# Folding w_phi into key weights by tiles of 64 rows and 64 columns, in a two-layer Hedgehog and Mish kernel

## Chip, cores and metric

The kernel runs on 1 core of one Trainium2 chip, in float32. The metric is the device time of one execution in microseconds. A matmul whose operands have the type fp32r stands in the trace as one record; one with plain float32 operands stands as two.

## The reference

Two layers, each an attention block and a dense block, on x of 2048 rows and 640 columns. Attention has 32 heads of 20.

```python
q, k, v = layernorm(x) @ wqkv                      # 32 heads of 20 each
pq = einsum("bhsd,hdf->bhsf", q, w_phi);  pk = the same of k
phi_q = concat(softmax(pq), softmax(-pq));  phi_k = the same of pk
kv = phi_k^T v;  z = sum of phi_k
x = x + (phi_q kv / (phi_q z + 1e-6)) @ wo
x = x + mish(layernorm(x) @ w1 + b1) @ w2
```

## The kernel before

Rows are worked in 8 blocks of 256 (two tiles of 128). To keep precision with fp32r matmuls, weights and activations are split into a high part (ScalarE copies to fp32r) and a low part (another engine subtracts), and each product is three matmuls: high by high, high by low, low by high (`project_half`, L418).

At the start of layer one w_phi is folded into the query and key weights once, so that no block has to multiply by it: the transposed weight rows are the stationary operand and w_phi, laid out as blocks on a diagonal, is the moving one. Of each head's 20 columns the last is subtracted from the other 19 first (`shift_phi`, on POOL), which a softmax does not see. The result lies in PSUM; `fold_high` copies it to the high weights on ACT, `fold_low` subtracts on DVE for the low weights. Query weights are folded first; the key weights (`fold_phi`) in two portions, ahead of the second values and ahead of the first keys of block 0, whose order is q0, v0, v1, k0, q1, k1.

`features` makes the features of a tile of queries or keys: copy from PSUM (ACT, L436 or L439), maximum and minimum (DVE, L443), the difference to the maximum (L444, on POOL for queries and on DVE for keys), the difference to the minimum (DVE, L446), exp (ACT, L449), the sums and reciprocals (DVE, L454, L455), and the scaling (POOL, L457). A query tile is then turned on DVE (L525) and stored to HBM in four pieces of e_d (SP, L528). Query tiles lie in two buffers by turns, so query i + 2 may be written only when the stores of query i have landed; the first to write is the MEMSET of L434 on POOL.

All DMAs are issued by SP, in its order. Each engine's order comes from a scheduler, held in part by `tc.issue_after`. In block 0 of layer one, waiting generators are moved on by `advance`; `last_fold` holds the last subtraction of the fold.

Of the kernel before, what the change touches and what calls it, by code (L numbers as in the profile page):

```python
# [16 lines left out]
P = 128  # L17
# [27 lines left out]
def kernel(  # L45
# [22 lines left out]
    def mm_tile():  # L68
        return psum.tile([P, 2, 512], F32, tag="mm", name="mm", bufs=2)
# [179 lines left out]
    def load_raw(which, ts=range(6)):  # L249

        raw = []
        for t in ts:
            rows = 120 if t < 4 else 80
            if t < 5:
                r = wts.tile([P, D], F32, tag=f"r2{'hl'[which]}{5 + t}", name=f"raw{which}{t}")
            else:
                r = r2_wide(10 + which, F32)[:, 0]

            n = P if t < 5 else rows
            c0 = which * D + (t * 120 if t < 5 else D - rows)  # L260
            nc.sync.dma_start(r[:n], wqk_t[c0:c0 + n, :])
            raw.append((r, rows))
        return raw
# [26 lines left out]
        last_fold[0] = nc.vector.tensor_tensor(ws[k][1][:, cs], ps[:, :cs.stop - cs.start],  # L290
                                               ws[k][0][:, cs].bitcast(F32), op=ALU.subtract).ins

    def fold_phi(ws, bd, raw, parts):

        for n in range(0, len(parts), 2):
            mm = mm_tile() if n < 4 else None
            pair = list(zip(parts[n:n + 2], [one_tile(), one_tile()] if mm is None else [mm[:, 0], mm[:, 1]]))
            with tc.issue_after(last_product[0]):
                for (k, c), ps in pair:
                    for t in range(3 * c, 3 * c + 3):  # L300
                        fold_part(ps, k, t, bd, raw)
            for end in (fold_high, fold_low):
                for (k, c), ps in pair:
                    end(ws, ps, k, c)


    def norm_stats(t, xt):

# [158 lines left out]
    def attend_first(layer, x_src, first):  # L467
# [46 lines left out]

        def queries(xts, i, ps=None):
            e = query_tile(i)
            yield from features(project(xts, i % BT, q_ws, 0, w=QC) if ps is None else ps, e, True)

            b, t = divmod(i, BT)
            if i == NT - BT - 1:  # L520
                yield
                with tc.issue_after(last_recip[0]):
                    nc.vector.transpose(e, e)
            else:
                nc.vector.transpose(e, e)  # L525
            dst = e_d[b].rearrange("(j f) (t q s) -> t q f j s", f=32, t=BT, s=32)
            for q in range(4):
                ins = nc.sync.dma_start(dst[t, q], e[32 * q:32 * q + 32].rearrange("f (j s) -> f j s", s=32))  # L528
                last_store[0] = ins.ins
                if b == NB - 1:  # L530
                    yield
# [15 lines left out]
        if first is None:  # L547
            with written():
                xt = fetch(x_src, 0)
                bd = big_tile()[:120, :720].rearrange("p (t c) -> p t c", t=6)  # L550
                nc.sync.dma_start(bd[:, :3], phi_bd[:, :3])
                raw_q = load_raw(0, range(3))

                nc.vector.memset(bd[:80, 5, :80], 0.0)
                nc.sync.dma_start(bd[:40, 5, :40], phi_bd[80:120, 4, 80:120])
                nc.sync.dma_start(bd[40:80, 5, 40:80], phi_bd[:40, 5, :40])
                nc.sync.dma_start(bd[:, 3:5], phi_bd[:, 3:5])
                shift_phi(bd, slice(0, 3))
                raw_q += load_raw(0, range(3, 6))
                kv_ws = [r1_pair(k) for k in range(KD)]  # L560
                raw_v = [fetch_v(k) for k in range(KD)]
                raw = load_raw(1)
                early = fetch(x_src, 1)
                mvs = [norm_stats(t, xt) for t in range(BT)]
                norm_scale(0, mvs)
                shift_phi(bd, slice(3, 5))
                shift_phi(bd, 5)

                q_ws = [r2_pair(k) for k in range(KD)]
                mm = [mm_tile(), mm_tile()]  # L570
                pcs = [one_tile(), mm[0][:, 0], mm[0][:, 1], mm[1][:, 0], mm[1][:, 1]]
                for t in range(3):
                    for k in range(KD):
                        fold_part(pcs[k], k, t, bd, raw_q)
                xn = [row_tile() for _ in range(BT)]
                act(xn[0], xt[:, 0, :], AF.Identity, bias=stats[:, 0, 1, 0:1], scale=stats[:, 0, 0, 0:1])
                nc.vector.tensor_scalar(xn[1], xt[:, 1, :], stats[:, 0, 0, 1:2], stats[:, 0, 1, 1:2],
                                        op0=ALU.mult, op1=ALU.add)

                def highs(c, ks):  # L580
                    for k in ks:
                        fold_high(q_ws, pcs[k], k, c)

                def lows(c, ks):
                    for k in ks:
                        fold_low(q_ws, pcs[k], k, c)

                def make_v(k, low):
                    split(kv_ws[k][0][:, D:2 * D], kv_ws[k][1][:, D:2 * D], raw_v[k], low)

                def half(c, ks):
                    project_half(q0[c], nxt, 0, q_ws, 0, c, ks, w=QC)

                highs(0, (0, 1, 2))
                lows(0, (0,))
                nxt = Transposed(xn)
                nxt.turn(one_tile())
                nxt.high()
                lows(0, (1, 2))
                nxt.lower()  # L600
                highs(0, (3, 4))
                pcs[0], pcs[1] = one_tile(), one_tile()
                for k in (0, 1):
                    fold_part(pcs[k], k, 3, bd, raw_q)
                nxt.turn(one_tile())
                for t in (4, 5):
                    for k in (0, 1):
                        fold_part(pcs[k], k, t, bd, raw_q)
                last = mm_tile()
                nxt.turn(last[:, 0])  # L610
                nxt.high()
                nxt.high()
                lows(0, (3, 4))
                nxt.lower()
                nxt.lower()
                highs(1, (0, 1))
                q0 = [one_tile()]
                half(0, (0, 1))
                mm = mm_tile()
                pcs[2], pcs[3] = mm[:, 0], mm[:, 1]  # L620
                for k in (2, 3):
                    for t in range(3, 6):
                        fold_part(pcs[k], k, t, bd, raw_q)
                lows(1, (0, 1))
                half(0, (2, 3))
                make_v(0, nc.gpsimd)
                highs(1, (2, 3))
                lows(1, (2, 3))
                pcs[4] = last[:, 1]
                for t in range(3, 6):  # L630
                    fold_part(pcs[4], 4, t, bd, raw_q)
                half(0, (4,))
                make_v(1, nc.gpsimd)
                highs(1, (4,))
                lows(1, (4,))
                q0.append(one_tile())
                half(1, range(KD))
                for k in (2, 3, 4):
                    make_v(k, nc.vector)
            nc.sync.dma_start(mask, bass.AP(tensor=head_mask.tensor, offset=head_mask.offset,  # L640
                                            ap=[[1, 120], [120 * (DH + 1), 3]]))
        else:
            nxt, kv_ws, turn = first
            with tc.issue_after(last_load[0]):
                load_k_weights(kv_ws)
            q_ws = load_q_weights()
        for b in range(NB):
# [15 lines left out]
            for n, (kind, t) in enumerate(order):  # L663
                t = int(t)
                i = b * BT + t
                if b == 0 and layer == 0 and n in (2, 3):
                    if n == 2:
                        advance()
                    fold_phi(kv_ws, bd, raw, ((0, 0), (1, 0), (2, 0), (3, 0)) if n == 2 else
                             ((4, 0), (0, 1), (1, 1), (2, 1), (3, 1), (4, 1)))  # L670
                if b == 0 and n == (1 if layer else 3):
                    kva = one_tile()
                    nc.vector.memset(kva[:, :360], 0.0)
# [13 lines left out]
                if b == 0 and not layer:  # L687
                    with tc.issue_after(last_product[0]):
                        next(g)
                    with (tc.issue_after(last_fold[0]) if n > 3 else nullcontext()):  # L690
                        advance()
                    if n == 1:
                        xt = fetch_normed(1)
                elif b == NB - 1 and n == 3:
                    advance()
                    next(g)
                else:
                    next(g)
                    if layer and b == 0 and n == 0:
                        turn()  # L700
                    advance()
# [449 lines left out]
```

## Time and profile before

| | us |
|---|---|
| median of 3 runs | 1353.56 (1352.92 to 1353.92) |
| the profiled execution | 1354.08 |
| its span, first to last instruction | 1352.1 |
| PE busy | 1346.0 |
| DVE busy | 1040.4 |
| ACT busy | 576.6 |
| POOL busy | 480.6 |

The granted TensorE clock was 1.000 of full speed. In a timeline row the columns are: start and busy time in us, engine, line, operation, what it writes and reads, shape, count, and in brackets the idle time of the engine before it and what ended it. A row of the table by windows gives the stretch, its length, the busy time of each engine with its count of instructions (PE, PEld, DVE, ACT, POOL), the granted clock, the DMA engines' mean busy share and GB/s. A row of waits gives the engine, its tile and line, what it waited for, the sum in us, the number and the longest.

### The profile page before, as it was taken

How to read it: one execution, taken by the hardware profiler on the slowest of the kernel's cores; microseconds unless marked ns; L12 is line 12 of the kernel's file. 1: busy time of each engine (PE TensorE's matmuls, PEld its weight loads, DVE VectorE, ACT ScalarE, POOL GpSimd, SP SyncE). 2: the span in 40 equal slices, each digit the busy share in tenths (PEclk: the TensorE clock that was granted, in tenths of full speed). 3: DMA queues.
4: the chain of work that ended last, by engine and by line, in shares of the span. 5: the costliest groups of instructions: out<-in, count | busy, mean ns of one | idle time of the engine just before them, and what ended most of it. 6: DMA issues, size and time to landing. Idle time of an engine off the chain costs nothing. (4 is left out here: it accounts for less than half of the span.)

```text
span 1352.1 us, 31029 instructions
## 1 busy us (share of the span) xinstructions
PE 1346.0 (100%) x12896; PEld 1337.5 (99%) x12896; DVE 1040.4 (77%) x1737; ACT 576.6 (43%) x974; POOL 480.6 (36%) x479
## 2 busy tenths in 40 slices
PE   9999999999999999999999999999999999999999
PEld 9999999999999999999999999999999999999998
DVE  6888888876787877778768788789768776676775
ACT  5444444222454554445443334332236444444443
POOL 3365554434322222222226655634351211111112
PEclk9999999999999999999999999999999999999999
DMA  9554444698713443234474444548974221233200
GB/s 334 165 119 103 99 99 102 170 287 284 214 25 87 117 118 78 61 98 113 144 221 108 113 97 90 95 95 270 278 253 121 79 73 38 87 98 98 65 35 21
DMA packets 352694, 174.12 MB, mean 129 GB/s; under 512 B 287513, under 2 KB 324105, under 8 KB 352553
## 3 DMA queue, kind: packets, MB, share of 16 engines
q1 hardware_dynamic: 352553, 172.14, 46.6%
q8 instruction: 101, 1.65, 0.5%
q14 instruction: 40, 0.33, 0.1%
HBM read 106.23 MB, written 65.86 MB: 127 GB/s over the span
## 5 line engine op out<-in xcount | busy, mean ns | idle before, releaser
L952 POOL TENSOR_TENSOR ol<-big,ol 128x512 fp32r<-128x512 f32 (+1 forms) x98 | 131.9, 1346 | 471.8 <-ACT ol L951 406.1
L977 PE MATMUL mm<-r2h,ol 128*128 128x320 f32 x1240 | 296.1, 309 | 0.0
L926 PE MATMUL one<-xtl,r1h 128*128 128x256 f32 x960 | 268.2, 279 | 0.0
L926 PE MATMUL one<-xth,r1l 128*128 128x256 f32 x960 | 268.0, 279 | 0.0
L926 PE MATMUL one<-xth,r1h 128*128 128x256 f32 x960 | 265.8, 279 | 0.0
L977 PEld LDWEIGHTS mm<-r2h,ol 128*128 128x128 f32 x1240 | 212.4, 188 | 0.0
L977 PE MATMUL mm<-r2l,ol 128*128 128x320 f32 x620 | 191.2, 309 | 0.0
L418 PE MATMUL mm<-r1h,xth 128*128 128x304 f32 (+1 forms) x600 | 184.9, 308 | 1.1 <-ACT r L135 1.1
L418 PE MATMUL mm<-r1h,xtl 128*128 128x304 f32 (+1 forms) x600 | 183.8, 306 | 0.2 <-POOL xtl L355 0.2
L418 PE MATMUL mm<-r1l,xth 128*128 128x304 f32 (+1 forms) x600 | 184.0, 307 | 0.0
L926 PEld LDWEIGHTS one<-xtl,r1h 128*128 128x128 f32 x960 | 180.4, 188 | 0.0
L926 PEld LDWEIGHTS one<-xth,r1l 128*128 128x128 f32 x960 | 180.4, 188 | 0.0
L926 PEld LDWEIGHTS one<-xth,r1h 128*128 128x128 f32 x960 | 179.6, 188 | 0.0
L941 DVE TENSOR_SCALAR big<-big 128x512 f32<-128x512 f32 (+1 forms) x98 | 55.4, 565 | 121.2 <-ACT big L939 116.8
L939 ACT ACTIVATE big<-one,b1s 128x256 f32<-128x256 f32 x192 | 80.9, 468 | 101.4 <-PE one L926 101.2
L951 ACT ACTIVATE ol<-big 128x512 fp32r<-128x512 f32 (+1 forms) x98 | 60.9, 622 | 136.5 <-DVE big L950 136.4
L457 POOL TENSOR_TENSOR r<-r,r 128x1280 f32<-128x1280 f32 x32 | 77.4, 2420 | 112.3 <-DVE r L455 88.9
L977 PEld LDWEIGHTS mm<-r2l,ol 128*128 128x128 f32 x620 | 116.4, 188 | 0.0
L943 ACT ACTIVATE big<-big,two 128x512 f32<-128x512 f32 (+1 forms) x98 | 70.1, 715 | 105.5 <-DVE big L942 105.4
L418 PEld LDWEIGHTS mm<-r1h,xth 128*128 128x128 f32 x600 | 112.8, 188 | 2.0 <-ACT r L135 1.4
L418 PEld LDWEIGHTS mm<-r1h,xtl 128*128 128x128 f32 x600 | 112.8, 188 | 0.3 <-POOL xtl L355 0.3
L418 PEld LDWEIGHTS mm<-r1l,xth 128*128 128x128 f32 x600 | 112.8, 188 | 0.1
(167 smaller groups left out, 3138.5 us busy)
## 6 DMA issues: line engine op xcount, KB each, us to landing
e_d<-r SPq DMA_DIRECT2D x128, 160.0 KB, 4.0
big<-e_d SPq DMA_DIRECT2D x30, 640.0 KB, 7.5
x_d<-xt SPq DMA_DIRECT2D x23, 640.0 KB, 5.0
xt<-x_d SPq DMA_DIRECT2D x22, 640.0 KB, 4.7
n_d<-xn SPq DMA_DIRECT2D x168, 80.0 KB, 2.2
xt<-in_x SPq DMA_DIRECT2D x16, 640.0 KB, 4.9
xn<-x_d SPq DMA_DIRECT2D x28, 320.0 KB, 4.5
v<-n_d SPq DMA_DIRECT2D x30, 256.0 KB, 3.0
```

The lines of the kernel that those rows point to most:

```text
L418: last_product[0] = nc.tensor.matmul(ps[:, :w], a[:, sl], r, start=(k == 0 and n == 0), stop=(k == KD - 1 and n == 2)).ins
L457: ins = scale.tensor_tensor(eg, eg, r.unsqueeze(2).to_broadcast([P, 2 * H, DH]), op=ALU.mult).ins
L926: nc.tensor.matmul(ph[:, j, :], l, r, start=(n == 0), stop=(n == 3 * KD - 1))
L939: exps[0] = nc.scalar.activation(part(ta, 0)[:, j - js.start], ph[:, j, :], AF.Exp, bias=b1s[:, 2 * pr + j:2 * pr + j + 1]).ins
L941: nc.vector.tensor_scalar_min(e, e, E_CAP)
L943: nc.scalar.activation(r, n, AF.Ln, bias=two)
L951: nc.scalar.activation(ah[:, js], n, AF.Copy)
L952: nc.gpsimd.tensor_tensor(al[:, js], n, ah[:, js].bitcast(F32), op=ALU.subtract)
L977: ins = nc.tensor.matmul(pys[t][c][:, :HC], (ah, ah, al)[n][:, j, t * P:(t + 1) * P], w, start=(f == 0 and n == 0), stop=(f == KF - 1 and ...
```

## The change

Four edits. First, the key rows are loaded shifted by 4 rows, so that three heads lie in partitions 4 to 63 and three in 64 to 123, and w_phi is loaded a second time in that layout (`load_phi_halves`), with zeros in rows 0 to 3, and subtracted by `shift_phi`. Second, `fold_keys` takes the place of `fold_phi`: 22 products for each of five k, each of at most 64 rows by 64 columns, the two row halves into different PSUM banks, the column halves into different partitions; a k is evacuated with one instruction over both banks and one for the last two heads (three for k = 4). Third, in block 0 the `advance` at n = 3, which turns query 0, is placed behind the last subtraction of the fold. Fourth, in layer two L444 of query tile 2 (the first of block 1) is done by DVE.

```diff
-            n = P if t < 5 else rows
-            c0 = which * D + (t * 120 if t < 5 else D - rows)
+            if which:
+                n = P if t < 5 else 64
+                c0 = D + (120 * t - 4 if t < 5 else D - n)
...
+    def load_phi_halves():
+
+        ph = pair_tile(F32).rearrange("p a s -> p (a s)")[:, :360].rearrange("p (t c) -> p t c", t=6)
+        nc.vector.memset(ph, 0.0)
+        for s in range(2):
+            nc.sync.dma_start(ph[4 + 60 * s:64 + 60 * s, :5], phi_bd[60 * s:60 * s + 60, :5, 60 * s:60 * s + 60])
+        nc.sync.dma_start(ph[24:64, 5, :40], phi_bd[:40, 5, :40])
+        return ph
+
+    def fold_keys(ws, ph, raw, ks):
+
+        w = 3 * DL
+        for k in ks:
+            mm = mm_tile() if k < KD - 1 else None
+            ps = [one_tile(), one_tile()] if mm is None else [mm[:, 0], mm[:, 1]]
             with tc.issue_after(last_product[0]):
+                for t in range(6):
+                    heads = 3 if t < 5 else 2
+                    for s in range(2 if t < 5 else 1):
+                        rows = slice(64 * s, 64 + 60 * s)
+                        for c in range(2):
+                            last_product[0] = nc.tensor.matmul(
+                                ps[s][64 * c:64 * c + 64, t * w:t * w + heads * DL].rearrange("p (j d) -> p j d", d=DL),
+                                raw[t][0][rows, k * P + 64 * c:k * P + 64 * c + 64],
+                                ph[rows, t, :heads * DH].rearrange("p (j d) -> p j d", d=DH)[:, :, :DL],
+                                start=True, stop=True).ins
...
+            outs.append((ps[0][:, 5 * w:5 * w + 2 * DL], *ends))
+            for src, hi, lo in outs:
+                nc.scalar.activation(hi, src, AF.Copy)
+            for src, hi, lo in outs:
+                last_fold[0] = nc.vector.tensor_tensor(lo, src, hi.bitcast(F32), op=ALU.subtract).ins
...
-            yield from features(project(xts, i % BT, q_ws, 0, w=QC) if ps is None else ps, e, True)
+            yield from features(project(xts, i % BT, q_ws, 0, w=QC) if ps is None else ps, e, not layer or i != BT)
...
                 raw = load_raw(1)
+                ph = load_phi_halves()
                 early = fetch(x_src, 1)
...
                     make_v(k, nc.vector)
+                shift_phi(ph, slice(0, 6))
...
-                    fold_phi(kv_ws, bd, raw, ((0, 0), (1, 0), (2, 0), (3, 0)) if n == 2 else
-                             ((4, 0), (0, 1), (1, 1), (2, 1), (3, 1), (4, 1)))
+                    fold_keys(kv_ws, ph, raw, (0, 1) if n == 2 else (2, 3, 4))
...
-                    with (tc.issue_after(last_fold[0]) if n > 3 else nullcontext()):
+                    with (tc.issue_after(last_fold[0]) if n > 2 else nullcontext()):
                         advance()
```

The diff moves line numbers by 29 or 30 from `features` on: L444 becomes L473, L446 L475, L457 L486, L525 L554, L528 L557.

On DVE, behind the statistics of block 1 (r1l are the low key weights, r_361 and r_367 query 0), before:

```order
L454 TENSOR_REDUCE r<-r_361 128x64
L290 TENSOR_TENSOR r1l_167<-mm,r1h_166 128x342
L290 TENSOR_TENSOR r1l_169<-mm,r1h_168 128x342
L455 RECIPROCAL r<-r 128x64
L290 TENSOR_TENSOR r1l_171<-mm,r1h_170 128x342
L290 TENSOR_TENSOR r1l_173<-mm,r1h_172 128x342
L525 STREAM_TRANSPOSE r_361<-r_361 128x1280
L673 MEMSET one 128x360
L290 TENSOR_TENSOR r1l_175<-mm,r1h_174 128x342
```

and after, from the subtractions of k = 2 on:

```order
L334 TENSOR_TENSOR r1l_171<-mm,r1h_170 128x2x5x57
L334 TENSOR_TENSOR r1l_171<-mm,r1h_170 128x38
L703 MEMSET one 128x360
L334 TENSOR_TENSOR r1l_173<-mm,r1h_172 128x2x5x57
L334 TENSOR_TENSOR r1l_173<-mm,r1h_172 128x38
L334 TENSOR_TENSOR r1l_175<-one,r1h_174 128x5x57 x2
L334 TENSOR_TENSOR r1l_175<-one,r1h_174 128x38
L554 STREAM_TRANSPOSE r_367<-r_367 128x1280
```

The turn of query 0 has moved behind all subtractions of the fold.

On SP, where the folded weights are stored (wp_d) and wo is loaded, before:

```order
L164 DMA raw_1069<-in_wo 128x640
L464 DMA xt<-in_x 128x1280
L528 DMA e_d_116<-r_361 32x40x32 x4
L230 DMA wp_d<-r1h_166 128x608
L230 DMA wp_d<-r1l_167 128x608
```

and after, from the last key weights that are stored before the queries:

```order
L164 DMA raw_1159<-in_wo 128x640
L164 DMA raw_1155<-in_wo 128x640
L230 DMA wp_d<-r1h_174 128x608
L230 DMA wp_d<-r1l_175 128x608
L557 DMA e_d_116<-r_367 32x40x32 x4
L493 DMA xt<-in_x 128x1280
```

The four stores of query 0 stand behind all ten stores of key weights and the two further loads of wo.

On POOL, after (r_670 is query 1, r_820 query 2, ol the halves of w_phi):

```order
L463 MEMSET r_367 128x32
L463 MEMSET big 128x32 x2
L282 TENSOR_TENSOR ol<-ol 128x18x19
L473 TENSOR_TENSOR r_367<-r_367,m 128x32x20
L349 TENSOR_SCALAR ve<-mv 128x1 x2
L350 TENSOR_TENSOR stats<-ve,neg_half 128x2
L352 TENSOR_SCALAR stats<-mv,stats 128x1 x2
L486 TENSOR_TENSOR r_367<-r_367,r 128x1280
L463 MEMSET r_670 128x32
L463 MEMSET r_820 128x32
L473 TENSOR_TENSOR r_670<-r_670,m 128x32x20
```

The subtraction on the halves is new, ahead of the first query's difference; the MEMSETs of queries 1 and 2 stood ahead of query 1's difference before too.

More of the change, by code (lines that the diff above doesn't have):

```diff
@@ L257, in load_raw @@
                 r = r2_wide(10 + which, F32)[:, 0]
-            n = P if t < 5 else rows
-            c0 = which * D + (t * 120 if t < 5 else D - rows)
+            if which:
+                n = P if t < 5 else 64
+                c0 = D + (120 * t - 4 if t < 5 else D - n)
+            else:
+                n = P if t < 5 else rows
+                c0 = t * 120 if t < 5 else D - rows
             nc.sync.dma_start(r[:n], wqk_t[c0:c0 + n, :])
@@ L291, in fold_low @@
                                                ws[k][0][:, cs].bitcast(F32), op=ALU.subtract).ins
[L293 to L297, printed above, removed]
-            with tc.issue_after(last_product[0]):
[L299 to L304, printed above, removed]
+    def load_phi_halves():
[5 more added lines that the diff above has]
+        return ph
@@ new lines, in fold_keys @@
+    def fold_keys(ws, ph, raw, ks):
[3 more added lines that the diff above has]
+            ps = [one_tile(), one_tile()] if mm is None else [mm[:, 0], mm[:, 1]]
+            with tc.issue_after(last_product[0]):
+                for t in range(6):
[8 more added lines that the diff above has]
+                                start=True, stop=True).ins
+            pairs = [x[:, :10 * w].rearrange("p (t s d) -> p s t d", s=2, d=w) for x in ws[k]]
+            ends = [x[:, 10 * w:QK] for x in ws[k]]
+            if mm is None:
+                outs = [(ps[s][:, :5 * w].rearrange("p (t d) -> p t d", d=w), *(x[:, s] for x in pairs))
+                        for s in range(2)]
+            else:
+                outs = [(mm[:, :, :5 * w].rearrange("p s (t d) -> p s t d", d=w), *pairs)]
+            outs.append((ps[0][:, 5 * w:5 * w + 2 * DL], *ends))
[3 more added lines that the diff above has]
+                last_fold[0] = nc.vector.tensor_tensor(lo, src, hi.bitcast(F32), op=ALU.subtract).ins
```

## The prediction

> **What bounds the kernel now.** I read the head of the page first, then the table of what TensorE waited for, then the timelines of all engines around the two stretches that the diff touches.
>
> ```profile
> span 1352.1 us, 31029 instructions
> PE 1346.0 (100%) x12896; PEld 1337.5 (99%) x12896; DVE 1040.4 (77%) x1737; ACT 576.6 (43%) x974; POOL 480.6 (36%) x479
> ...
> PE mm L418 <- ACT r L135: 1.1, 1, 1.1
> PE mm L418 <- POOL xtl L355: 0.2, 1, 0.2
> ```
>
> TensorE is the bound: it is busy for 1346.0 of 1352.1 us, and inside the program it waits for other engines in only two places worth a word, 1.1 and 0.2 us, both in layer two. So there are three ways to move the time: fewer microseconds of matmuls, the end of those waits, or a new wait. The rest of the kernel matters only by its slack.
>
> **The fold on TensorE.** Before, the 30 products of the key fold stand as 60 records in two stretches.
>
> ```profile
> 24.23 2.83 PE L270 MATMUL mm<-big,raw 120*128 120x114 f32 x24
> 26.83 0.39 PE L418 MATMUL one<-r1h,xth 128*128 128x320 f32 x1
> ...
> 31.31 1.24 PE L270 MATMUL mm<-big,raw 120*128 120x114 f32 x10
> ...
> 35.28 0.60 PE L338 MATMUL one<-ident,xn 128*128 128x128 f32 x4
> 35.64 0.38 PE L418 MATMUL mm<-r1h,xth 128*128 128x304 f32 x1
> ```
>
> They take 26.83 - 24.23 = 2.60 and 35.28 - 31.31 = 3.97 us, 6.57 together. After, there are 110 products of 64 rows by 64 columns with 57 moving columns (38 in the last), 220 records. The nearest rows are the products that already use tiles of columns.
>
> ```profile
> 71.95 1.48 PE L511 MATMUL one<-big,ol 128*21 128x40 f32 x128
> 73.36 0.42 PE L418 MATMUL mm<-r1l,xth 128*128 128x320 f32 x1
> ...
> 246.72 1.39 PE L802 MATMUL mm<-kvb,big 120*64 120x63 f32 x40
> 247.93 0.27 PE L802 MATMUL mm<-kvb,ol 80*64 80x42 f32 x4
> ```
>
> L802, two tiles of 64 columns with 63 moving columns, starts 40 records in 1.21 us: 60 ns for a pair. L511, four tiles, starts 128 records in 1.41 us: 11 ns for one. So tiles side by side overlap; tiles one below the other occur in no row. If they overlap too, each k costs ten groups of four and two pairs, 12 x 60 ns = 0.72 us, and five cost 3.6 us. About 0.2 us for each of the two changes of tile shape (an estimate) leaves a saving of 2.6 us. If they don't, 110 pairs at 60 ns are 6.6 us and nothing is saved. I take the first, since L511 shows that four can be in flight.
>
> The Trainium skill, "TensorE: Matmul & The Clock Gate", section "Wait — 56ns, not 53.3ns?", says that starts of small matmuls never come closer than about 25 ns. By that rule 220 records would take 5.5 us and the saving would be 1.1 us; the 11 ns of L511 disagree, and the measurement decides.
>
> **What the first key projection then waits for.** The saving counts only if L418 at 35.64 can start earlier. New on its path are three loads of w_phi in halves, the subtraction on them (`shift_phi`, POOL), and their place: on POOL the subtraction stands ahead of the first query's L444, and the loads stand between the key rows and the x tile of block 1.
>
> ```profile
> 44.00:48.00 4.00, 4.00 (x32) 4.00 (x31) 3.03 (x6) 0.95 (x2) 1.28 (x1) 1.00 1.02 376
> ...
> 5.45 0.76 POOL L278 TENSOR_TENSOR big<-big 120x342 f32<-120x342 f32 x1 [4.16 <-DMA big<-in_phi_bd]
> ...
> 21.86 1.28 POOL L444 TENSOR_TENSOR r<-r,m 128x640 f32<-128x640 f32 x1 [0.59 <-DVE m L443]
> ...
> 24.59 1.67 DVE L311 BATCH_NORM_STATS2 bn<-xt 128x6 f32<-128x320 f32 x4 [0.59 <-DMA xt<-in_x]
> ...
> 26.43 1.43 DVE L454 TENSOR_REDUCE r<-r 128x64 f32<-128x1280 f32 x1
> 27.78 0.92 DVE L290 TENSOR_TENSOR r1l<-mm,r1h 128x342 fp32r<-128x342 f32 x2
> ...
> 24.14 0.77 ACT L135 ACTIVATE ol<-one 128x320 f32<-128x320 f32 x2 [3.45 <-PE one L418]
> ...
> 27.09 0.80 ACT L286 ACTIVATE r1h<-mm 128x342 fp32r<-128x342 f32 x2 [0.34 <-PE mm L270]
> 28.11 1.74 ACT L135 ACTIVATE xn<-xt,stats 128x640 f32<-128x640 f32 x2 [0.21 <-POOL stats L323]
> ```
>
> The x tile (640 KB, 1.7 us at the 376 GB/s of the loaded queue) landed at 24.59, so the key rows ahead of it landed near 22.9. The halves come as 640 small pieces; I give them 0.6 us (estimate), so they land at 23.5. The subtraction takes 0.76, L444 starts at 24.3 instead of 21.86 and ends at 25.6, L446 behind it at 26.4, and only then come the statistics of block 1: 1.8 us later than 24.59. Their second aggregate now stands behind L454 (1.43), so the normalization xn goes from 28.11 to about 31.2 and ends at 33.0. ACT is in order: the copies of the second values (0.77) and then the high part of k = 2 (608 columns as before, 0.7) end near 34.5, its low part on DVE (0.8) at 35.3. The projection at 35.64 takes the PSUM buffer that this low part frees, so it starts at 35.3: a gain of 0.3, not 2.6. Bounds: loads 1 us earlier or later give 1.3 or -0.7; TensorE alone gives 2.6.
>
> The Trainium skill, "TensorEngine Tiling (Array Packing)", section "PSUM Bottleneck", says that tiling speeds up TensorE but not the emptying of PSUM, which may become the bottleneck. By the rule 0.3 and without it 2.6 us; no run here shows this fold yet.
>
> **The first query's turn behind the lows.** DVE's transpose L525 of query 0 moves behind ten subtractions, and on SP its four stores to e_d move from ahead of ten stores of key weights and two loads to behind all of them. What waits for these stores is not obvious: query 2 uses query 0's buffer, so its MEMSET waits on POOL for the last store, and behind that MEMSET on POOL stands L444 of query 1.
>
> ```profile
> 33.25 5.22 SPq L528 DMA_DIRECT2D e_d<-r  x4
> ...
> 47.20 1.55 SPq L164 DMA_DIRECT2D raw<-in_wo  x2
> ...
> 68.40 3.38 SPq L528 DMA_DIRECT2D e_d<-r  x4
> ...
> 41.62 0.17 POOL L434 MEMSET r<- 128x32 f32 x1 [5.88 <-DMA e_d<-r]
> ...
> 48.91 0.81 DVE L446 TENSOR_TENSOR r<-m,r 128x640 f32<-128x640 f32 x1
> ...
> 66.93 1.45 DVE L525 STREAM_TRANSPOSE r<-r 128x1280 f32<-128x1280 f32 x1
> ...
> 75.11 0.68 ACT L135 ACTIVATE r<-mm 128x608 f32<-128x608 f32 x1 [6.14 <-DMA e_d<-r]
> ...
> 77.28 0.30 PE L418 MATMUL mm<-r1h,xth 128*128 128x304 f32 x1
> ...
> 48.91:66.93 18.02, 18.02 (x131) 18.01 (x130) 18.02 (x23) 10.06 (x13) 8.81 (x8) 1.00 0.22 75
> 51.00:52.00 1.00, 1.00 (x9) 1.00 (x8) 1.00 (x2) 0.01 (x1) 0.90 (x2) 1.00 0.17 67
> 52.00:54.00 2.00, 2.00 (x16) 2.00 (x15) 2.00 (x3) 0.63 (x2) 0.45 (x2) 1.00 0.00 0
> ```
>
> When do the stores land now? Before, the MEMSET ran at 41.62, 8.4 us after the first store was issued. SP's work from 33.25 to 48.75 stays the same but the 5.22 us of stores come last, from 43.5; 8.4 later is 51.9, and the new loads add 0.6. The queue was drained at 52, so with the same bytes the last landing is not before 51.5. It is later if the stores, in a full queue, are issued slower; I allow 3 us, to 55.5. I take the middle: M = 53.5.
>
> From there the chain is fixed. The MEMSET and L444 take 0.1 + 1.28, so L446 of query 1 starts at M + 1.4 instead of 48.91. From L446 to query 1's L525, DVE was busy for 18.02 of 18.02 us: a queue without a gap, so all of it moves along, L525 to M + 19.4. From L525 to ACT's copy of query 3, which waits for the stores of query 1, it was 75.11 - 66.93 = 8.2 us, and the copy takes 0.7 with its hand-over. That copy frees the PSUM buffer of the first key projection of block 2 (77.28): M + 28.3 = 81.8. TensorE stands still until then, 4.5 us behind the profile before; the 0.3 us of the fold are swallowed by it. Before, this place had 77.28 - 75.8 = 1.5 us of slack, which is why no wait shows there. Bounds: M = 51.5 gives 2.5, M = 55.5 gives 6.5.
>
> **One query of layer two on DVE.** POOL gives up L444 of query 2 (block 1).
>
> ```profile
> 745.11 1.27 POOL L444 TENSOR_TENSOR r<-r,m 128x640 f32<-128x640 f32 x1
> ...
> 746.42 0.82 DVE L446 TENSOR_TENSOR r<-m,r 128x640 f32<-128x640 f32 x1 [5.69 <-POOL r L444]
> ...
> 760.61 1.50 DVE L525 STREAM_TRANSPOSE r<-r 128x1280 f32<-128x1280 f32 x1
> ...
> 762.13 8.15 SPq L528 DMA_DIRECT2D e_d<-r  x8
> ...
> 768.80 0.68 ACT L135 ACTIVATE r<-mm 128x608 f32<-128x608 f32 x1 [6.23 <-DMA e_d<-r]
> ...
> 769.54 0.41 PE L418 MATMUL mm<-r1h,xth 128*128 128x304 f32 x1 [1.10 <-ACT r L135]
> 771.69 0.39 PE L511 MATMUL one<-big,ol 128*21 128x40 f32 x18
> ```
>
> DVE stood idle for 5.69 us for POOL. Doing the 0.8 us itself, it starts L446 near 741.5, and L525, now also ahead in DVE's order, some 4 us sooner; the stores and the copy at 768.80 need only 1.3 us to end TensorE's wait. That is worth 1.2 us; the 0.2 us wait for xtl goes, and the 64 products that were split in two (18 records, then the rest) stand together, which saves one change of shape, 0.2. Sum 1.6 us; bounds 0 and 1.8. DVE, which takes on the 0.8 us, is covered by its own idle time.
>
> **Sum.** 4.5 - 1.6 = +2.9 us. The profiled execution took 1354.08 us with a span of 1352.1, 0.5 above the median of the runs, 1353.56; set on the median the forecast is 1356.5 us. Its own range is M's: 0.9 to 4.9, so 1354.5 to 1358.5.
>
> **Rivals.** *Not slower:* the stores of query 0 land in time. For it: the copy at 75.11 has 1.5 us of slack, and DMA engines may serve small stores between large ones. Against it: SP issues in order and the queue is full until 51. It decides at M = 48.9, where M + 28.3 meets 77.28. Then 0.3 and 1.6 us remain as gains, 1351.7; if the fold's 2.6 came through whole, 1349.4. Chance 0.16. *Layer two keeps its wait* because the stores there wait for something else: the change doesn't do what it says, 1.6 us dearer, 1358.1. Chance 0.08. *A second stall behind the first*: POOL and DVE come out of the new wait about 5 us late and TensorE 4.5, so a place with less than 0.5 us of slack stalls again; another 2 us, 1358.5 to 1360. Chance 0.08. That row tiles don't overlap costs nothing while the stall at 77 stands. The forecast keeps 0.68.
>
> **The numbers.** 0.2% (2.7 us, about what a measurement of this kernel can tell from no change) lies inside the forecast's range: 56% of it is above, so slower 0.38 + 0.16 = 0.54; within 0.30 + 0.08 = 0.38; faster 0.08, half of the first rival. The range leaves out most of that rival and little above: 1352.6 to 1359.6.
>
> **What would show it.** Right: a wait of PE L418 near 77 to 82 us for ACT r, 4 to 5 us long, behind an ACT copy released by DMA e_d<-r; the POOL MEMSET of query 2 near 53; the fold's records about 15 ns apart; no PE wait near 768. Wrong: the MEMSET before 49, no wait of PE before 100 us, or a wait in layer two as before.

## The result, and the profile after

The changed kernel takes 1358.77 us (median of 8 executions, 1355.70 to 1360.33) against 1353.85 for the kernel before (8 executions, 1352.92 to 1354.77): 4.9 us slower. The ratio of the mean times is 1.0032, with a 95% interval of 1.0021 to 1.0043. The forecast was 1356.5, range 1352.6 to 1359.6. What is new beside the median is the spread: 4.6 us from fastest to slowest, against 1.9 before. The profiled execution is the fastest of the eight, 1355.70, so it shows the mechanism but not its usual size; a second profile further down does.

The head of the page and the table of what TensorE waited for, after:

```profile
span 1353.9 us, 31360 instructions
PE 1343.6 (99%) x13056; PEld 1334.1 (99%) x13056; DVE 1040.2 (77%) x1740; ACT 576.0 (43%) x975; POOL 482.3 (36%) x479
...
PE one L540 <- POOL big L486: 2.5, 2, 1.7
PE mm L447 <- ACT r L135: 1.4, 1, 1.4
...
PE mm L447 <- DVE r1l L334: 1.0, 1, 1.0
...
```

TensorE is busy 2.4 us less than before and the span is 1.8 us longer: the fold's saving is there, and waits outweigh it. Layer two's two waits of before (1.1 and 0.2 us) are gone from the table. The timelines of the engines around the fold, in order of time:

```profile
23.02 0.76 POOL L282 TENSOR_TENSOR ol<-ol 128x342 f32<-128x342 f32 x1 [2.30 <-DMA ol<-in_phi_bd]
23.73 1.28 POOL L473 TENSOR_TENSOR r<-r,m 128x640 f32<-128x640 f32 x1
23.83 0.81 PE L318 MATMUL mm<-ol,raw 64*64 64x57 f32 x40
24.46 0.21 PE L318 MATMUL mm<-ol,r 64*64 64x38 f32 x2
...
25.35 0.41 PE L447 MATMUL one<-r1h,xth 128*128 128x320 f32 x1
...
34.74 0.38 PE L447 MATMUL mm<-r1h,xth 128*128 128x304 f32 x1 [0.95 <-DVE r1l L334]
```

Forty records start within 0.63 us, 16 ns apart, and two k take 25.35 - 23.83 = 1.52 us. Row tiles overlap. But the first key projection waits for the last subtraction of its PSUM buffer and starts at 34.74, only 0.90 us earlier than before (35.64). These 0.90 us hold a difference in when the fold began. Counted from the fold's own first record, the first key projection came 11.41 us later before (24.23 to 35.64) and comes 10.91 us later now: the new fold itself is worth 0.50 us. The rows of the later stall:

```profile
50.94 0.16 POOL L463 MEMSET r<- 128x32 f32 x1 [17.83 <-DMA e_d<-r]
51.01 1.28 POOL L473 TENSOR_TENSOR r<-r,m 128x640 f32<-128x640 f32 x1
52.33 0.83 DVE L475 TENSOR_TENSOR r<-m,r 128x640 f32<-128x640 f32 x1 [4.23 <-POOL r L473]
70.24 1.45 DVE L554 STREAM_TRANSPOSE r<-r 128x1280 f32<-128x1280 f32 x1
72.88 1.48 PE L540 MATMUL one<-big,ol 128*21 128x40 f32 x128 [1.75 <-POOL big L486]
79.01 0.68 ACT L135 ACTIVATE r<-mm 128x608 f32<-128x608 f32 x1 [8.82 <-DMA e_d<-r]
79.74 0.41 PE L447 MATMUL mm<-r1h,xth 128*128 128x304 f32 x1 [1.38 <-ACT r L135]
89.65 1.48 PE L540 MATMUL one<-big,v 128*21 128x40 f32 x128 [0.79 <-POOL big L486]
```

POOL stood 17.83 us before query 2's MEMSET, for the stores of query 0 (landed at 50.9, before: 41.6). From there on everything is late, and TensorE waits three times. The first key projection of block 2 starts at 79.74 instead of 77.28. In layer two the shift of TensorE's starts against the kernel before falls from 3.4 us (at 724 us) to 1.8 (at 802).

### The profile page after: what moved, and what is told of

The parts are those of the page before. It is cut to its first block, busy times and chain, and to the rows that moved or that the text cites. A ratio compares the mean times of both kernels' runs of the same rounds, so it can differ in the third digit from the quotient of the medians.

```text
span 1353.9 us, 31360 instructions
## 1 busy us (share of the span) xinstructions
PE 1343.6 (99%) x13056; PEld 1334.1 (99%) x13056; DVE 1040.2 (77%) x1740; ACT 576.0 (43%) x975; POOL 482.3 (36%) x479
## 4 chain that ended last, share of the span: by engine, by line
PE 90%; DVE 2%; POOL 1%; DMA 1%; issue 0%; SPq 0%; ACT 0%; POOLq 0%; DVEq 0%
PE one L956 25%; PE mm L1007 24%; PE mm L447 22%; PE one L447 12%; PE mm L832 3%; PE one L367 2%; PE one L540 1%; PE one L1007 1%; DMA e_d<-r 1%; DVE m L472 1%; PE one L832 1%; DVE r L475 1%; DVE r L483 0%; POOL big L486 0%; SPq L557 0%
## 5 line engine op out<-in xcount | busy, mean ns | idle before, releaser
L971 DVE TENSOR_SCALAR big<-big 128x512 f32<-128x512 f32 (+1 forms) x98 | 55.5, 567 | 121.7 <-ACT big L969 117.2
L486 POOL TENSOR_TENSOR r<-r,r 128x1280 f32<-128x1280 f32 x32 | 77.6, 2424 | 111.7 <-DVE r L484 73.1
```

Source lines behind the costliest of these rows:

```text
L486: ins = scale.tensor_tensor(eg, eg, r.unsqueeze(2).to_broadcast([P, 2 * H, DH]), op=ALU.mult).ins
L971: nc.vector.tensor_scalar_min(e, e, E_CAP)
```

## The experiments

Theory A: the loss comes from query 0's late stores, through the MEMSET that waits for them on POOL. Its rival, theory B: it comes from the fold's own order and evacuation. A third, C, arose on the way: some stalls of TensorE are waits for its own code. The kernels were timed in four sets, each on one chip together with the kernel before: 89 executions of it, 1352.61 to 1355.49, medians of the sets 1353.75 to 1354.01, granted clock 1.000 in every one.

**The changed kernel once more.** No edit; a second profile.

> The changed kernel once more, for a second profile. Theory A (late stores): the 4.6 us between its fastest and slowest execution come from the landing of query 0's four stores in a full DMA queue. The first profile (1355.7 us) had the POOL MEMSET of query 2 at 50.94; if this profile's execution takes 1355.7 + d, its MEMSET stands at 50.94 + d, within 0.7 us, and the three new waits of TensorE at 72.9, 79.7 and 89.7 us grow by d in sum. Theory B (the fold's own order): the MEMSET stays at 51 whatever the time, and d lies in other places. Median 1358.0 to 1359.5.

Measured: 1358.57 us (1356.69 to 1359.91), ratio 1.0035 (1.0022 to 1.0047); the profiled execution took 1358.87, span 1357.1. POOL, TensorE, and the table by windows:

```profile
53.00 0.16 POOL L463 MEMSET r<- 128x32 f32 x1 [18.90 <-DMA e_d<-r]
...
24.82 0.81 PE L318 MATMUL mm<-ol,raw 64*64 64x57 f32 x40 [0.89 <-POOL ol L282]
...
35.73 0.38 PE L447 MATMUL mm<-r1h,xth 128*128 128x304 f32 x1 [0.95 <-DVE r1l L334]
...
74.94 1.48 PE L540 MATMUL one<-big,ol 128*21 128x40 f32 x128 [2.83 <-POOL big L486]
82.23 0.41 PE L447 MATMUL mm<-r1h,xth 128*128 128x304 f32 x1 [1.79 <-ACT r L135]
...
92.79 1.48 PE L540 MATMUL one<-big,v 128*21 128x40 f32 x128
...
80.00:82.00 2.00, 0.43 (x3) 0.17 (x2) 0.04 (x1) 0.50 (x1) 0.47 (x2) 1.00 0.03 3
82.00:84.00 2.00, 1.77 (x10) 1.77 (x11) 1.72 (x3) 2.00 (x5) 2.00 (x2) 0.84 0.15 45
84.00:86.00 2.00, 2.00 (x9) 2.00 (x9) 2.00 (x4) 0.95 (x2) 2.00 (x3) 0.50 0.12 39
86.00:88.00 2.00, 2.00 (x13) 2.00 (x13) 2.00 (x5) 0.00 (x0) 2.00 (x3) 0.81 0.35 133
```

The expectation is half right. The MEMSET is later, by 2.06 us, but the execution is 3.17 us longer. The halves of w_phi landed later too, so the fold itself waited 0.89 us and the first key projection came at 35.73, again 10.91 us behind the fold's first record. And behind the stall stands what no expectation had: TensorE's granted clock (third column from the right) falls to half, and 0.16, 0.50 and 0.19 of three windows of 2 us are 1.70 us lost. The shift of TensorE's starts shows it too. The key projection is 4.95 us behind the kernel before (82.23 against 77.28), the L540 behind it 6.59 (92.79 against this row of before):

```profile
86.20 1.48 PE L511 MATMUL one<-big,v 128*21 128x40 f32 x128
```

That is 1.64 us more. In the first profile, at full clock, the same stretch added 0.99 us (2.46 to 3.45), mostly because L540 waited for POOL there (0.79 us). So of the 3.17 us between the two profiles 2.06 stand before the MEMSET, 0.43 in the landing of query 1's stores behind it (ACT's copy at 79.01 and 81.50), and only 0.65 are the net price of the half clock. Of the 14 executions of the changed kernel in the two sets 11 have a mean granted clock below 1.000; 1355.70, the first profile, is one of the three that have not.

**One MEMSET moved.** Query 2's MEMSET is queued behind query 1's difference on POOL:

```diff
-        nc.gpsimd.memset(eh[:, 1, :, DL:], 0.0)
+        with (tc.issue_after(subs[True]) if hold else nullcontext()): nc.gpsimd.memset(eh[:, 1, :, DL:], 0.0)
```

`hold` is set for query tile 2 of layer one, and `subs[True]` is POOL's last L473. In the traces all engines run the same instructions in the same order as in the changed kernel, but for this swap on POOL.

> The changed kernel with one POOL instruction moved: query 2's MEMSET stands behind query 1's difference L473 instead of ahead of it; nothing else moves on any engine. Theory A: L473 of query 1 no longer waits for the stores and starts near 46 us instead of 51.0; the TensorE waits at 72.9, 79.7 and 89.7 us (1.9 + 1.5 + 0.95 = 4.4 us over the usual start) go; what is left against the kernel before is the fold's 0.9 and layer two's 1.6 us: 1351.6 us, and executions within 1 us of each other. Rival: POOL's statistics of block 2 now stand behind the waiting MEMSET and take over the wait, 1353.5 to 1355. Theory B: no change, 1358.8.

Measured: 1352.84 us (1352.07 to 1355.68), ratio 0.9994 (0.9985 to 1.0003). POOL, and the whole table of TensorE's waits behind the warm-up:

```profile
46.56 1.28 POOL L473 TENSOR_TENSOR r<-r,m 128x640 f32<-128x640 f32 x1 [12.43 <-DVE m L472]
53.28 0.16 POOL L463 MEMSET r<- 128x32 f32 x1 [5.44 <-DMA e_d<-r]
...
PE mm L447 <- DVE r1l L334: 1.0, 1, 1.0
PE mm L318 <- POOL ol L282: 0.8, 1, 0.8
PE one L367 <- ACT ol L135: 0.5, 1, 0.5
PE mm L318 <- DVE r1l L334: 0.2, 1, 0.2
```

The stores land as late as ever, 53.28, and it costs nothing: L473 runs at 46.56 and the three waits are gone. One instruction's place on POOL is worth 5.7 us (1358.57 - 1352.84, same set). 1.2 us are missing to the expected 1351.6. In the profile 1.0 of them stand at the first projection, which comes at 35.76 instead of 34.74, since the halves came late here too (0.8 us).

**Layer two.** The changed kernel with `e, True` again, and the kernel before with the fourth edit alone:

```diff
-            yield from features(... if ps is None else ps, e, not layer or i != BT)
+            yield from features(... if ps is None else ps, e, True)
```

> The changed kernel with POOL doing the difference of query 2 in layer two again. If that edit is worth what the shift of TensorE's start shows (3.42 us behind the kernel before at 724 us, 1.82 behind at 802 us), this is 1.6 us slower than the changed kernel, near 1360.4, and TensorE waits 1.1 us for ACT's copy near 773 us again. Rival: the 1.6 us are a matter of the shifted start of layer two and not of the edit: then the same time as the changed kernel, 1358.8.

> The kernel before with the fourth edit alone (layer two, query 2's difference on VectorE). The sum of the prediction says 1.6 us less: 1352.3, with no TensorE wait at 769.5 us and a new one of about 0.3 us near 743 for xtl. Rival (the gain needs the later start of layer two): 0 to 0.5 us less, 1353.3 to 1353.9.

Measured: 1360.80 us (1357.94 to 1364.49), ratio 1.0054 (1.0040 to 1.0067), and 1352.36 (1351.67 to 1353.15), ratio 0.9989 (0.9980 to 0.9997). TensorE in the first, at layer two's query copy, and in the second:

```profile
780.39 0.41 PE L447 MATMUL mm<-r1h,xth 128*128 128x304 f32 x1 [1.58 <-ACT r L135]
```

```profile
743.52 0.41 PE L418 MATMUL mm<-r1h,xtl 128*128 128x304 f32 x1 [0.29 <-POOL xtl L355]
```

Without the edit the wait is back and the time 2.2 us longer than with it in the same set (few executions, 5, and a further stall in its profile, below); alone it is worth 1.65 us (1354.01 - 1352.36), with the small new wait for xtl. The forecast's 1.6 stands.

**The place of the turn.** The changed kernel with the turn ahead of the lows, the kernel before with the turn behind them:

```diff
-                    with (tc.issue_after(last_fold[0]) if n > 2 else nullcontext()):
+                    with (tc.issue_after(last_fold[0]) if n > 3 else nullcontext()):
```

(the second: the other way round.)

> The changed kernel without the third edit: query 0 is turned on VectorE ahead of the lows of k = 2, 3 and 4, and its stores stand on SP ahead of the key weights of k = 2 to 4 and of two loads of wo. Theory A: the stores land near 44, POOL's MEMSET no longer stops query 1, the waits of TensorE between 70 and 90 us go; the turn (1.5 us) delays the low part for which the first key projection waits, 34.74 + up to 1.5 = 36.2 at most, 0.6 behind the kernel before. So -1.6 + 0.6 at worst and -1.6 - 0.9 at best against the kernel before: 1351.3 to 1352.9, executions within 1 us. Theory B (the loss is the fold's): 1357 or more.

> The kernel before with the third edit alone. Here SP puts the four stores behind eight of ten key weight stores, and POOL puts query 2's MEMSET behind query 1's difference. Theory A, as the result has taught it (the order on POOL decides whether late stores cost): no stall behind the MEMSET; only the later turn, and the copy of query 2 if the stores land after 57: within 1 us of the kernel before, 1353 to 1355. The prediction's simpler form (late stores cost 4.5 us by themselves): 1358.

Measured: 1354.30 us (1352.91 to 1355.39), ratio 1.0002 (0.9994 to 1.0011), and 1353.63 (1352.76 to 1354.50), ratio 0.9998 (0.9990 to 1.0007). The first, POOL and TensorE:

```profile
24.93 0.76 POOL L282 TENSOR_TENSOR ol<-ol 128x342 f32<-128x342 f32 x1 [3.41 <-DMA ol<-in_phi_bd]
...
47.40 0.16 POOL L463 MEMSET r<- 128x32 f32 x1 [12.37 <-DMA e_d<-r]
...
37.36 0.38 PE L447 MATMUL mm<-r1h,xth 128*128 128x304 f32 x1 [1.66 <-DVE r1l L334]
```

The stall goes with the early turn: the MEMSET still stands ahead of the difference on POOL, but the stores land at 47.40, and TensorE does not wait behind it. The time is 1.4 us above the expected band. The profile is of the slowest of the eleven executions: in it the halves landed later than in any other, and the turn stands ahead of the low part, so the first projection came at 37.36, 1.7 behind the kernel before; TensorE stood 1.2 us at 324.5 for no engine (theory C, below); layer two gives 1.6 back. How much of this holds for the median isn't shown. The second, POOL:

```profile
45.24 1.28 POOL L444 TENSOR_TENSOR r<-r,m 128x640 f32<-128x640 f32 x1 [10.70 <-DVE m L443]
47.54 0.16 POOL L434 MEMSET r<- 128x32 f32 x1 [1.02 <-DMA e_d<-r]
```

Here the late turn is free. The scheduler happened to put the MEMSET behind the difference, but the stores also landed at 47.5, ahead of the 48.9 from which the prediction saw a loss, so this run does not show by itself that the order decides. The moved MEMSET does: there the stores landed at 53.28 and cost nothing.

**The fold alone.** The kernel before with the first two edits (the changed kernel with `n > 3` and `e, True`).

> The kernel before with the first two edits alone (the fold in tiles of 64 by 64, its shifted key rows and w_phi halves). From the runs so far: with the turn ahead of the lows the first key projection stood at 37.4 us instead of 35.6, of which 1.7 us was the late landing of the halves (subtracted at 24.9 instead of 23.0); layer two is as before. So 1.5 to 2.0 us slower than the kernel before, 1355.4 to 1355.9, though TensorE's products themselves take 3 us less. Rival (the fold is a gain and the turn ahead of the lows costs all of it): 1353.9 or less. Open beside it: whether TensorE's stall near 321 to 328 us without a waited-for engine, seen in three of seven profiles with this fold and in none of three without it, comes again.

Measured: 1355.97 us (1355.09 to 1359.71), ratio 1.0024 (1.0012 to 1.0035). TensorE:

```profile
35.71 0.38 PE L447 MATMUL mm<-r1h,xth 128*128 128x304 f32 x1 [1.66 <-DVE r1l L334]
323.12 0.42 PE L447 MATMUL one<-r2h,xtl 128*128 128x320 f32 x1 [1.50 <-issue]
```

The sum was met for a wrong reason: the first projection is as before (35.71 against 35.64), and the loss stands at 323 us, where TensorE waits 1.5 us for nothing that the table names. The expected 1.7 us at the first projection had been taken from an execution with very late halves. With the early turn the projection comes 11.61 us behind the fold's first record (24.10), 0.20 more than with the old fold: the new fold gains nothing there. Of the seven executions three have a mean clock below 1.000, among them the two slowest, 1358.02 and 1359.71. Alone, the three parts cost +2.2 us (fold), -0.2 (turn) and -1.65 (layer two), +0.3 in sum; the whole change costs 4.9. The difference is the stall behind the MEMSET with what follows it, and this needs the fold and the late turn together.

**The halves loaded first**, alone and with the MEMSET moved:

```diff
-                raw = load_raw(1)
                 ph = load_phi_halves()
+                raw = load_raw(1)
```

> The changed kernel with the loads of the w_phi halves issued ahead of the key rows. The chain of the prediction: the halves no longer hold POOL's L473 of query 0 (23.73 us), which starts near 21.3; the statistics of block 1 then start with the landing of its x tile at 24.6 instead of 25.8, and the first key projection at 33.5 instead of 34.74. This 1.2 us is lost again in the stall behind the late stores, unless these land earlier too: 1357.5 to 1358.8. Rival: the key rows land 0.6 us later and the fold with them, no gain at the first projection.

> Both: the halves loaded ahead of the key rows, and query 2's MEMSET behind query 1's difference on POOL. With the stall gone the earlier first projection counts in full: 1.2 us less than with the MEMSET moved alone, 1350.4. If something other than the landing of the halves sets the first projection, it is the same as with the MEMSET alone, 1351.6.

Measured: 1356.89 us (1355.66 to 1360.24), ratio 1.0026 (1.0015 to 1.0036), and 1351.95 (1350.51 to 1356.50), ratio 0.9988 (0.9979 to 0.9997). The first, POOL, VectorE and TensorE:

```profile
22.01 1.27 POOL L473 TENSOR_TENSOR r<-r,m 128x640 f32<-128x640 f32 x1 [0.59 <-DVE m L472]
...
25.43 1.67 DVE L340 BATCH_NORM_STATS2 bn<-xt 128x6 f32<-128x320 f32 x4 [1.28 <-DMA xt<-in_x]
...
34.48 0.39 PE L447 MATMUL mm<-r1h,xth 128*128 128x304 f32 x1
```

POOL no longer waits for the halves, but the x tile lands later than expected and bounds instead; the first projection gains 0.3 us on the first profile (expected 1.2) and 1.2 on the usual 35.7. The second, with the stall gone, has a median 0.9 us below the kernel with the MEMSET alone, but they were timed in different sets and the intervals of their ratios overlap. It is the lowest median found; its ratio is that of layer two alone (0.9989). Its executions spread over 6 us, and three of the eleven, two of the three slowest among them, have a mean clock below 1.000. In its profile, 1354.02 us, 1.65 us are lost where the fold alone had lost its 1.5:

```profile
322.79 0.42 PE L447 MATMUL one<-r2h,xtl 128*128 128x320 f32 x1 [1.65 <-issue]
```

**The stall without a releaser.** In the last row TensorE stands still and the profile names nothing that it waited for ("issue"). This stall stands before the same record of TensorE, the 3,924th, in four of eight profiles with the new fold and in none of four without. The trace's packets on the instruction queue, q8, are 16,384 bytes each; start and end of the one next to that record (us), and the starts of the records on both sides:

```
                                fetch              record before  record after
no stall
changed kernel, first profile   320.75 to 322.14   324.70         324.84
changed kernel, second profile  324.30 to 325.24   327.84         327.98
MEMSET moved                    317.55 to 318.96   321.38         321.53
halves first                    321.61 to 322.73   325.49         325.64
stall
halves first, MEMSET moved      320.56 to 321.51   320.84         322.79
turn ahead of the lows          322.01 to 322.91   322.99         324.52
without the layer-two edit      327.79 to 328.74   327.63         330.15
fold alone                      320.77 to 321.72   321.31         323.12
```

Where the fetch had ended 2.4 us or more before, there was no stall; where not, TensorE went on 1.3 to 1.6 us behind its end. The page counts 102 fetches for 26,112 instructions (13,056 matmuls, as many weight loads), 256 in each, so these packets are TensorE's code; the fold's 160 more records shift the later code by 320. That TensorE waited for the packet is read from these times; no record names it. Two kernels move that boundary with idle transposes in the warm-up, one without the fold and one with it:

```diff
-    for _ in range(30):
-        nc.tensor.transpose(warm[:, :P], ident, ident)
+    for m in [32] * 40 + [P] * 22:        # the other: [32] * 116 + [P] * 10
+        nc.tensor.transpose(warm[:m, :m], ident[:m, :m], ident[:m, :m])
```

The first goes on top of this one, the kernel before with the third and fourth edits:

> The kernel before with the third and fourth edits, without the fold. The two were worth -0.2 and -1.5 us alone, so -1.7 together: 1352.1. If the late turn costs in this order too (a stall near 73 to 82 us as in the changed kernel), 1354 or more. The stores land near 47.5 and query 2's MEMSET stands behind query 1's difference, so no stall is expected, and TensorE's granted clock stays 1.000 in all executions.

Measured: 1352.25 us (1351.56 to 1352.78), ratio 0.9988 (0.9979 to 0.9997), as expected, every clock at 1.000. Then the shifts:

> The third and fourth edits on the kernel before, and in the warm-up at the start 40 transposes of 32 by 32 and 22 of 128 by 128 in place of 30 of 128 by 128: 64 more TensorE instructions (a weight load and a matmul each), which do nothing but move all later code by a quarter of one 16 KB fetch of 256 instructions. The fold's 160 more records moved it by 320 instructions, the same but for one whole fetch. Theory C (the stall at 321 to 328 us is TensorE waiting for its code): the stall comes in here too, in about half of the executions, and these spread over 2 us or more, against 1.2 us without the shift; median 1352.5 to 1353.5. Rival (the stall belongs to the fold's data or to its DMAs): the spread stays at 1.2 us, and the time at 1352.2 plus what the longer warm-up costs (0 to 1 us).

> The kernel with all four edits, query 2's MEMSET moved and the halves loaded first, and in the warm-up 116 transposes of 32 by 32 and 10 of 128 by 128 in place of 30: 192 more TensorE instructions, with which the fetches fall in the later code as in the kernel before. Theory C: the stall near 321 us goes, the executions spread over 2 us at most (6.0 without the shift), and the median falls to the fastest of those, 1350.5 to 1351.2, plus what the longer warm-up costs. Rival: the spread stays near 6 us and the median at 1352.

Measured: 1353.84 us (1352.60 to 1357.53), ratio 1.0004 (0.9995 to 1.0013), and 1353.12 (1352.16 to 1353.74), ratio 0.9994 (0.9985 to 1.0003). The spreads move as theory C says, and both ways: without the fold 1.2 us become 4.9, with it 6.0 become 1.6. The 4.9 rest on one execution, 1357.53; the other ten spread over 2.2. The medians do not follow: they rise by 1.6 and 1.2 us. The longer warm-up delays the first product from 6.68 to 7.95 us in the one and from 6.78 to 9.82 in the other, but of that only 0.9 and 0.6 us are left at the first key projection (34.81 to 35.71, 35.23 to 35.81), so a part of the rise is not explained. The profile of the first caught no stall (its execution was the second fastest), so that the stall returned there is inferred from the times alone. The profile of the second has no stall without a releaser, but one of 0.5 us for VectorE at 302 us that no other has. The case for theory C is the order in time in the eight profiles above; the shifts support it and do not prove it.

## Why the forecast came out as it did

**The sum.** Forecast: 4.5 - 1.6 = +2.9. Measured: +4.9. The second profile, close to the median, adds up: the key projection of block 2 is 82.23 - 77.28 = 4.95 us late, nearly all of it by the two waits ahead of it (2.83 and 1.79), the stretch at half clock costs 1.64, layer two gives 1.6 back; together +5.0, and the span is 1357.1 against 1352.1.

**The stall: right.** The MEMSET was forecast at 53.5, bounds 51.5 and 55.5; the four profiles with the late turn and the MEMSET ahead of the difference have 50.94, 51.77, 53.00 and 53.50. L475 at M + 1.4, L554 at M + 19.3 and the key projection at M + 28.8 to 29.2 follow the chain (forecast 1.4, 19.4, 28.3). The one wait foreseen came as two or three: TensorE stops first for POOL's L486, which comes late by the same chain.

**The step that fell short** is "TensorE stands still until then, 4.5 us behind". At the M of the second profile, 53.0, it gives 4.0 us. Measured are 4.95, as the chain from M took 29.2 us and not 28.3, and then 1.64 more behind the key projection, which the sum put at nothing. In the second profile these are the half clock, which was in no row of the kernel before and in no rival; 11 of 14 executions have a mean clock below 1.000. In the first profile, at full clock, they are 0.99 us, with the third wait for POOL: that is the rival "a second stall behind the first", at half its price. The range was drawn from M alone. It holds the result, but M was met within 0.5 us in the second profile, and the missing 2 us came from these other terms; that is luck.

**The fold: mechanism right, size off.** Row tiles overlap (two k in 1.52 us; five at that rate 3.8, forecast 3.6), and the evacuation and the halves, not TensorE, set the first projection. The gain was put at 0.3, bounds 1.3 and -0.7; the four profiles with the late turn and the halves behind the key rows show 0.9, -0.1, -0.1 and -0.5 against 35.64. Counted from the fold's first record all four have 10.91 us, and the four without the new fold 11.41 or 11.42: a gain of 0.50, less what the fold's start loses by waiting for the halves (0.8 to 1.3 us in three of the four). Without the new fold the first key projection came between 34.45 and 35.66, so a single profile could not have told. The Trainium skill's least 25 ns between starts ("TensorE: Matmul & The Clock Gate", "Wait — 56ns, not 53.3ns?") does not hold for these tiles, 16 ns. The Trainium skill, "TensorEngine Tiling (Array Packing)", "PSUM Bottleneck", has the emptying of PSUM as what may bind once tiles speed TensorE up; the 0.95 us wait for L334 agrees. A price of 320 more instructions was not in the sum: if theory C holds, it is 1.2 to 2.2 us of waiting for code in half of the profiles with the fold, though in neither of the changed kernel's own two.

**Layer two: right**, 1.6 forecast, 1.65 alone.

**Not slower and the other rivals.** "Not slower" would have needed M below 48.9; with the late turn no profile came near. Two other ways led there: the early turn, with M at 47.40 (ratio 1.0002), and, with stores as late as 53.28, the MEMSET's other place (ratio 0.9994).

## What to carry to other kernels

Before a store is moved later, look on which in-order engine the next writer of its buffer is queued, and what stands behind that writer: here the place of a MEMSET of 0.16 us, ahead of work that did not need it, was worth 5.7 us, more than the whole loss. Price an idle stretch of TensorE with the half-clock stretch that may follow, less the waits that a slower TensorE no longer meets. When times spread, take the profile of a second execution, and count from the start of the work that was changed: what stands ahead of it differs by up to a microsecond between executions. More, smaller instructions also mean more code fetches, and a stall that seems to be one showed far from the change.

## What the runs showed that was not expected

**Half clock can follow a stall of two to three microseconds.** The changed kernel without the layer-two edit, TensorE's rows behind two stalls and the table by windows there:

```profile
75.44 2.60 PE L540 MATMUL one<-big,ol 128*21 128x40 f32 x128 [2.93 <-POOL big L486]
...
330.15 0.41 PE L447 MATMUL one<-r2h,xtl 128*128 128x320 f32 x1 [2.21 <-issue]
...
75.00:78.00 3.00, 2.56 (x129) 2.45 (x129) 3.00 (x5) 0.00 (x0) 0.55 (x2) 0.50 0.83 129
...
330.00:334.00 4.00, 3.85 (x16) 3.85 (x17) 0.35 (x1) 0.00 (x0) 0.00 (x0) 0.58 0.71 252
```

Half clock follows a wait for POOL of 2.93 us and the unnamed one of 2.21. Behind the second it costs about 1.7 us (0.42 of 4 us in the last row). Behind the first it costs the key projection nothing, since that waits for ACT's copy in any case: it starts 29.2 us behind the MEMSET (53.50 to 82.72), as in the second profile. The Trainium skill, "TensorE: Matmul & The Clock Gate", "Part 1: The HAM clock gate", has free-running windows of about 3.4 us and half speed after an idle one; 1.7 us lost at half speed agree with that length, but a whole idle window is more than was needed. A wait of 2.84 us in another kernel (the halves loaded first) was not followed by half clock:

```profile
73.72 1.48 PE L540 MATMUL one<-big,ol 128*21 128x40 f32 x128 [2.84 <-POOL big L486]
```

The clock records of the traces show where the stalls fall. The stretches between two changes of the clock are whole multiples of 3.41 us: 78.51 us is 23 of them in the second profile, 68.27 is 20 and 252.59 is 74 here. In these steps TensorE was idle for 2.10 and 2.21 us of the 3.41 just ahead of the two half clocks above, while the 2.84 us were divided, 1.1 in one step and 1.7 in the next. But idle time in a step does not decide alone: in the second profile 1.79 us were followed by half clock and 1.83, two steps earlier, were not. What decides stays open. Nor does half clock need the stall behind the MEMSET: with the turn ahead of the lows 6 of 11 executions have a mean clock below 1.000, though that stall is gone.

**A stall beside a code fetch.** The Trainium skill, "Runtime: NRT & Kernel Launch", "Instruction fetch mechanics", has the same blocks of 256 instructions and calls their fetch hidden; here TensorE stood 1.2 to 2.2 us at one place in four of eight profiles, and went on 1.3 to 1.6 us behind the end of such a fetch.
